# The channel table loaded in six pieces, and a new list of steps

## The chip, the cores and the metric

The kernel runs on one core of a Trainium2 chip. The metric is the device time of one execution in microseconds (us). Three executions of the kernel before took 529.64, 529.9 and 531.75 us; the median is 529.9 us.

## The reference

The reference is a gated linear attention (HGRN2) followed by a Fourier mixing block with a two-layer MLP. There are four batches, eight heads of 48 channels and 768 tokens; the eight heads make 384 channels.

```python
f = 1.0 / (1.0 + np.exp(-f_logit))
for t in range(S):
    state = f[:, :, t, :, None] * state + np.einsum('bhd,bhe->bhde', k[:, :, t], v[:, :, t])
    y[:, :, t] = np.einsum('bhd,bhde->bhe', q[:, :, t], state)
# heads side by side: x is (batch, 768, 384)
X = np.fft.fft(np.fft.fft(x, axis=1), axis=2)
u = x + np.real(X)
un = (u - mean(u)) / np.sqrt(var(u) + 1e-06)
out = u + np.maximum(un @ w_ch1, 0.0) @ w_ch2     # 384 -> 1536 -> 384
```

## The kernel before

**Work and stages.** Two heads make one unit, so there are 16 units, four to a batch. A unit runs through twelve or thirteen steps of the generator `attention`: the gate on ScalarE (L372, L373), a scan over the tokens on VectorE that gives the tile `W` (L379), exponentials on ScalarE (L383, L384, L387), two products on VectorE that turn q and k into scaled queries and keys (L391, L392), scores on TensorE (L400), a masked copy `at` on VectorE (L404), values and state sums `ds` on TensorE (L559, L599), a short scan `stt` over the chunk states on VectorE (L607), the state's part of the output (L616), a transpose back (L636), and `fold` on VectorE, which writes the even and odd parts `eo` (L663 to L669). The third and fourth unit of a batch also form the operands of the cosine transform there (`xs`, `xc`, `se`, `ce`, L678 to L687).

When the four units of a batch are folded, `fnet` does the Fourier transform with cosine and sine matrices: four products `z` with the sequence table `tab` (L725), then `mid` and `mix` with the channel table `cd` (L759, L744), and VectorE adds the result to x and takes the moments (L761 to L803). `turns` normalises a block of 128 tokens (`un`, L780) and transposes it (`pt`, L783; `unT`, L784), and `projected` does the MLP: for batch 0 with plain products `up` (L865) and `po` (L874), for the later batches with a fast matrix scheme (L836, L843), both followed by products `fx`, `fz` (L888). The tiles of `z`, `mid`, `mix`, `pt`, `up` and `po` share two PSUM buffers.

**Weights.** The MLP's weights arrive as 64-bit numbers in 24 blocks. `fetch` loads a block into one of three `raw` buffers (L310), and `weights` makes single precision of it with one instruction on ScalarE (L281), two on VectorE (L283, L284) and one on GpSimd (L285).

**What sets the order.** All steps stand in one list of words, `ORDER`, which a loop goes through (L951); each word issues its instructions to their engines' queues at once, and every queue then runs in that order. The scheduler adds only the waits. The words are: a bare number for the next step of that unit; `L` for loads of a unit (`L4qv`: q and v of unit 4); `K` for the turned keys of a unit; `r` for one fetch and `R` for three; `C` for one conversion of weights; `D` for eight filler matmuls on TensorE (L192); `T` for loading the tables and `S` for sorting them on GpSimd; `F`, `H` and `P` with a batch number for the next step of `fnet`, `turns` and `projected`; `B` and `W` for sums of weight blocks; `V` and `c` for a second look at the weights. `Z`, `I`, `i` and `M` set up and close.

**Loads.** All loads but the gather go through SyncE's queue. They take eight completion counters in turn, and a load whose counter is still in use waits, with all behind it, until the load eight before it has landed. A q, k or f load is 112 rows of 3 KB, issued as 96 and 16 rows; v is 360 KB and a weight block 384 KB. `tables` loads `tab` in four pieces (128, 15, 112 and 1 rows), has GpSimd gather its second half (L226, 395 KB), and loads the channel table into two tiles `wave` in three pieces. `sort_tables` then copies both into `cd` on GpSimd (L240 to L252).

```python
nc.sync.dma_start(out=wave[0][0:QD + 1], in_=dim_tab[0:QD + 1, 0])        # 97 rows, L232
nc.sync.dma_start(out=wave[1][0:63], in_=dim_tab[65:128, 1])              # 63 rows, L233
nc.sync.dma_start(out=wave[1][63:QD], in_=dim_tab[0:QD - 63, 2])          # 33 rows, L234
```

Of the kernel before, what the change touches and what calls it, by code (L numbers as in the profile page):

```python
# [12 lines left out]
C = 128  # L13
# [11 lines left out]


ORDER = (
    "Z I D L0f 0 i D L2f 2 D L1f D 1 L0q 0 L0k r D D D L1q 1 0 D D L0v L1k 0 L2q 2 C D 0 0 L2k 1 D D r 0 "
    "L3fk K0 D 1 1 K1 1 C 0 0 r 2 2 L1v D 3 D D r L3q 0 L2v L4fk 3 K2 C 1 0 C 1 1 3 2 1 D 2 3 3 4 2 0 L3v "
    "1 2 L5fk 5 D D 3 4 R 2 1 5 2 3 K3 C 4 3 L4qv 3 T D 2 L6fk 3 L5qv 5 C 4 D 2 4 4 3 3 4 S 2 3 C 5 K4 4 "  # L30
    "F0 F0 4 F0 F0 r C K5 5 6 r C 4 L6qv 5 F0 r r 4 5 L7fk H0 H0 r 5 H0 C 6 C 5 P0 7 P0 P0 r 6 C L7qv 6 "
    "P0 P0 5 C 6 K6 P0 r 6 7 C r P0 C P0 r r 7 C P0 F0 6 5 7 r r L9fk B C P0 P0 6 C 6 r r K7 C F0 P0 7 C "
    "7 C r 6 r H0 r C P0 P0 C 7 6 C P0 L8fk 7 H0 B L8qv 9 P0 P0 H0 B B 9 P0 8 7 P0 B 8 P0 9 B P0 P0 P0 8 "
    "P0 7 L9qv 4 9 9 K9 P0 B P0 5 8 P0 P0 7 H0 9 P0 7 9 8 B 9 H0 6 P0 P0 L11fk 9 11 W P0 6 P0 P0 9 K8 P0 "
    "P0 P0 B P0 P0 P0 P0 P0 8 7 P0 P0 P0 F1 P0 F1 L11qv P0 F1 F1 11 8 F1 P0 8 8 L10fk 10 P0 P0 P0 8 10 H1 "
    "P0 L10qv B P0 11 P0 P0 10 10 H1 B P0 P0 11 10 K10 P0 10 B 10 11 K11 11 L12fk B P0 H1 B B P1 P1 P1 P1 "
    "P1 B P1 P1 P1 P0 P1 P1 P1 P1 F1 P1 P1 F1 P1 P1 10 12 9 12 10 P1 P1 10 8 L12qv H1 9 P1 P1 12 12 10 P1 "
    "P1 H1 11 P1 12 11 H1 12 11 P1 P1 P1 H1 P1 P1 P1 P1 L13fk 13 P1 11 H1 P1 P1 P1 P1 P1 P1 P1 8 P1 P1 12 "
    "K12 L14fk 13 P1 14 P1 P1 12 L13qv 13 11 10 P1 13 12 10 P1 K13 11 P1 P1 P1 P1 P1 P1 14 P1 12 P1 11 P1 "
    "P1 P1 F2 F2 P1 14 P1 L14qv 14 F2 P1 P1 F2 P1 13 13 F2 13 K14 F2 F2 L15fk 13 13 P1 14 13 H2 P1 15 P1 "  # L40
    "15 P1 P1 L15qv 15 14 P1 14 P1 H2 14 15 H2 14 P1 P2 P2 P2 P2 H2 P2 P2 P2 P2 P2 P2 P2 P2 P2 P2 P2 13 "
    "14 15 H2 15 V 13 P2 K15 15 14 15 H2 V 14 15 P2 V P2 14 15 12 P2 P2 P2 15 12 c P2 H2 V P2 P2 P2 P2 P2 "
    "c 15 15 P2 P2 F3 F3 F3 P2 F3 P2 H2 P2 c P2 F3 P2 P2 F3 P2 c V F3 P2 P2 V P2 P2 P2 c c V V P2 P2 P2 "
    "H3 c P2 H3 P2 P2 P2 c P2 H3 P2 P2 P2 P2 P2 P2 P2 P2 V P2 P2 V P2 P2 P2 P2 V P2 P2 P2 c P2 c V c P2 V "
    "P3 c V P2 P3 P3 H3 V H3 P3 P3 P3 P3 P3 H3 P3 P3 P3 P3 P3 P3 P3 c V c c P3 c P3 V V P3 P3 P3 c P3 P3 "
    "P3 P3 P3 V P3 P3 H3 P3 P3 P3 P3 c c P3 V V V P3 P3 V P3 P3 P3 c c P3 P3 P3 P3 P3 P3 c V P3 P3 H3 c "
    "P3 c P3 P3 P3 M P3 P3 P3 P3 P3 P3 P3 P3 P3 P3 P3 P3 P3 P3 P3 P3 P3 P3 P3 P3"
)


# [33 lines left out]
def kernel(  # L84
# [13 lines left out]
    nc = tc.nc  # L98
    B, HP, _, D, _, S = qkf.shape
# [7 lines left out]
    QS, QD = S // 4, DM // 4  # L107
    R = 64 + D
# [106 lines left out]
    def tables():  # L215


        nc.sync.dma_start(out=tab[:, 0, 0], in_=seq_tab[:, 0, 0])
        nc.sync.dma_start(out=tab[1:16, 0, 1], in_=seq_tab[1:16, 0, 1])
        nc.sync.dma_start(out=tab[16:128, 0, 1], in_=seq_tab[16:128, 0, 1])  # L220
        nc.sync.dma_start(out=tab[0:1, 0, 1], in_=seq_tab[64:65, 1, 1])
        back = p1.tile([128, 1], U32, tag="most", name="back")
        nc.gpsimd.iota(back, pattern=[[0, 1]], base=1, channel_multiplier=3)
        nc.gpsimd.iota(back[64:128], pattern=[[0, 1]], base=3 * C + 1, channel_multiplier=-3)
        nc.gpsimd.iota(back[64:65], pattern=[[0, 1]], base=2, channel_multiplier=0)
        nc.gpsimd.indirect_dma_start(  # L226
            out=tab[:, 1].rearrange("p t m -> p (t m)"), out_offset=None,
            in_=seq_tab.rearrange("p j t m -> (p j) (t m)"),
            in_offset=bass.IndirectOffsetOnAxis(ap=back, axis=0))

        wave = [p2.tile([128, DM], F32, tag="un", name=f"wave{i}") for i in range(2)]
        nc.sync.dma_start(out=wave[0][0:QD + 1], in_=dim_tab[0:QD + 1, 0])  # L232
        nc.sync.dma_start(out=wave[1][0:63], in_=dim_tab[65:128, 1])  # L233
        nc.sync.dma_start(out=wave[1][63:QD], in_=dim_tab[0:QD - 63, 2])  # L234
        return wave

    def sort_tables(wave):
# [712 lines left out]
    with tc.manual_schedule():  # L950
        for word in ORDER.split():  # L951
            kind, n = word[0], int("0" + "".join(c for c in word if c.isdigit()))
# [14 lines left out]
            elif kind == "B":  # L967
                weight_sum()
            elif kind == "H":
                next(behind[n], None)  # L970
            elif kind == "r":
                fetch()
            elif kind == "V":
                reread()
            elif kind == "D":
                busy()
            elif kind == "C":
                weights()
            elif kind == "c":
                sizes()  # L980
            elif kind == "R":
                fetch(3)
            elif kind == "L":
                load(n, *word.strip("L0123456789"))
            elif kind == "I":
                start()
            elif kind == "i":
                nc.sync.dma_start(out=ident, in_=ident_in)
            elif kind == "T":
                wave = tables()  # L990
            elif kind == "S":
                sort_tables(wave)
            elif kind == "Z":
                zeros()
            elif kind == "M":
                flag = judge()
# [92 lines left out]
```

## Time and profile before

| What | Value |
|---|---|
| median of three executions | 529.9 us |
| the profiled execution's own time | 528.67 us |
| span of the profiled execution | 526.9 us |
| instructions | 13784 |
| TensorE (PE) busy | 497.4 us, 94% of the span |
| VectorE (DVE) busy | 379.6 us, 72% |
| ScalarE (ACT) busy | 224.8 us, 43% |
| GpSimd (POOL) busy | 58.0 us, 11% |
| moved by DMA | 48.15 MB, mean 91 GB/s |

The profiled execution is a fourth one; its span is 1.77 us shorter than its own time. Shares are means over a kernel with a loading stage, an attention stage and a long MLP stage, so they are read by stretches of time below, not as totals. In lines of a timeline the first number is the start, the second the duration (of a group: of the whole group), and the square brackets say how long the engine had stood idle before and what released it.

### The profile page before, as it was taken

What the parts mean: (1) busy time and instruction counts of PE and PEld (TensorE: products, weight loads), DVE (VectorE), ACT (ScalarE), POOL (GpSimd) and SP (SyncE); (2) the same over time, 40 slices, a digit from 0 to 9 for tenths busy, and PEclk for the clock granted to TensorE, in tenths of its full rate; (3) what the DMA queues carried; (4) which work ended last, traced back from release to release, by engine and by line L of the source; (5) the groups of instructions that cost most, each with busy time, mean ns of one, the idle gap of its engine ahead of it and who ended that gap; (6) DMA issues with size and microseconds to landing.
All of it is one profiled execution on the core that took longest, in us unless ns stands there. A gap on an engine that the chain in (4) does not pass through costs nothing.

```text
span 526.9 us, 13784 instructions
## 1 busy us (share of the span) xinstructions
PE 497.4 (94%) x5854; PEld 456.9 (87%) x5854; DVE 379.6 (72%) x746; ACT 224.8 (43%) x529; POOL 58.0 (11%) x85
## 2 busy tenths in 40 slices
PE   4867789999999999999999999999999999999995
PEld 4756668866899889999999889999899999999995
DVE  3777998998896258696598886686787566757561
ACT  6474667655530371444634534451441405132230
POOL 3110633351001000100001000000000000010000
PEclk9788899999999999999999999999999999999998
DMA  8998635674021121103031212110323112421101
GB/s 212 258 242 214 188 106 159 193 214 124 12 76 63 39 70 44 43 1 117 23 89 51 55 55 71 47 63 14 106 61 104 47 61 91 145 66 60 34 1 36
DMA packets 20462, 48.15 MB, mean 91 GB/s; under 512 B 3366, under 2 KB 5991, under 8 KB 20391
## 3 DMA queue, kind: packets, MB, share of 16 engines
q1 hardware_dynamic: 19142, 43.43, 29.5%
q0 software_dynamic: 1104, 3.54, 1.8%
q8 instruction: 48, 0.79, 0.6%
q14 instruction: 24, 0.19, 0.1%
q10 hardware_dynamic: 144, 0.20, 0.1%
HBM read 42.44 MB, written 4.72 MB: 89 GB/s over the span
## 4 chain that ended last, share of the span: by engine, by line
PE 81%; DVE 9%; issue 1%; ACT 1%; DVEq 0%
PE ub L836 24%; PE fx L888 16%; PE fz L888 12%; PE up L865 7%; PE z L725 3%; PE po L874 3%; PE y L559 3%; PE mix L744 2%; PE pt L783 2%; PE ds L599 2%; DVE w L284 2%; PE y L616 2%; PE yt L636 1%; PE sc L400 1%; PE st L538 1%
## 5 line engine op out<-in xcount | busy, mean ns | idle before, releaser
L843 DVE TENSOR_TENSOR h<-h,ub 128x512 f32<-128x512 f32 x81 | 55.1, 686 | 40.4 <-PE ub L836 40.3
L692 POOL DMA_INDIRECT out_dram<-x,place x16 | 17.8, 1112 | 383.5 <-DVE x L918 261.6
L841 ACT ACTIVATE h<-ub 128x512 f32<-128x512 f32 x54 | 32.2, 597 | 58.6 <-PE ub L836 58.1
L865 PE MATMUL up<-unT,w 128*128 128x256 f32 x216 | 49.3, 381 | 0.6 <-ACT unT L784 0.6
L845 ACT ACTIVATE h<-h 128x512 f32<-128x512 f32 x54 | 33.9, 631 | 33.3 <-DVE h L843 33.3
L888 PE MATMUL fx<-block,h 128*128 128x192 f32 x264 | 46.6, 327 | 0.0
L836 PE MATMUL ub<-unT,w 128*128 128x128 f32 x360 | 46.6, 280 | 0.0
L865 PEld LDWEIGHTS up<-unT,w 128*128 128x128 f32 x216 | 40.2, 190 | 6.3 <-ACT unT L784 0.8
L888 PE MATMUL fx<-w,h 128*128 128x192 f32 x264 | 45.4, 327 | 0.0
L836 PEld LDWEIGHTS ub<-unT,w 128*128 128x128 f32 x360 | 43.2, 191 | 0.7
L888 PEld LDWEIGHTS fx<-block,h 128*128 128x128 f32 x264 | 43.3, 190 | 0.1
L888 PEld LDWEIGHTS fx<-w,h 128*128 128x128 f32 x264 | 42.7, 190 | 0.3 <-ACT unT L784 0.2
L836 PE MATMUL ub<-wide 128*128 128x128 f32 x288 | 39.0, 281 | 0.0
L836 PE MATMUL ub<-wide,w 128*128 128x128 f32 x288 | 38.2, 280 | 0.0
L285 POOL TENSOR_TENSOR w<-w,raw 128x384 uint32<-128x384 uint32 x24 | 27.2, 1132 | 75.9 <-DVE w L284 39.1
L836 PEld LDWEIGHTS ub<-wide 128*128 128x128 f32 x288 | 34.6, 191 | 1.0 <-issue 0.4
L836 PEld LDWEIGHTS ub<-wide,w 128*128 128x128 f32 x288 | 34.3, 191 | 1.1 <-DVE h L843 0.3
L379 DVE TENSOR_TENSOR_SCAN W<-g,bound 112x768 f32<-112x768 f32 x12 | 21.0, 1750 | 9.2 <-ACT g L373 9.2
L784 ACT COPY unT<-pt 128x384 f32<-128x384 f32 x24 | 11.6, 487 | 35.8 <-PE pt L783 35.8
L867 ACT ACTIVATE h<-up 128x256 f32<-128x256 f32 x36 | 13.5, 380 | 30.3 <-PE up L865 30.3
L559 PE MATMUL y<-at,v 64*48 64x64 f32 (+1 forms) x768 | 19.3, 229 | 6.6 <-DVE at L404 2.9
L559 PEld LDWEIGHTS y<-at,v 64*64 64x64 f32 (+1 forms) x768 | 15.6, 135 | 10.3 <-issue 4.1
(188 smaller groups left out, 1003.0 us busy)
## 6 DMA issues: line engine op xcount, KB each, us to landing
raw<-in_w_ch_dram SPq DMA_DIRECT2D x24, 384.0 KB, 6.1
v<-in_v_dram SPq DMA_DIRECT2D x16, 288.0 KB, 4.5
k<-in_w_ch_dram SPq DMA_DIRECT2D x12, 384.0 KB, 3.7
g<-in_w_ch_dram SPq DMA_DIRECT2D x12, 384.0 KB, 3.4
k<-in_qkf_dram SPq DMA_DIRECT2D x14, 288.0 KB, 4.0
g<-in_qkf_dram SPq DMA_DIRECT2D x12, 288.0 KB, 6.4
q<-in_qkf_dram SPq DMA_DIRECT2D x12, 288.0 KB
wide<-in_qkf_dram SPq DMA_DIRECT2D x10, 288.0 KB, 5.4
```

The source lines that it names most:

```text
L285: nc.gpsimd.tensor_tensor(bits, bits, lo, ALU.add)
L379: nc.vector.tensor_tensor_scan(W, g, bound[:R], 0.0, ALU.add, ALU.min)
L559: nc.tensor.matmul(y[FILL[g], c // 3, c % 3 * C + t.start:c % 3 * C + t.stop], lhsT=vals[rows, o:o + (64 if g == 0 else D)], rhs=weights, ...
L692: nc.gpsimd.indirect_dma_start(out=out.rearrange("b s d -> (b s) d"), out_offset=bass.IndirectOffsetOnAxis(ap=place[:, b, i:i + 1], axis=0 ...
L725: nc.tensor.matmul(z[:, cols], lhsT=src[:, j, lo:hi], rhs=tab[:, t, T % 2, cols], start=(i == 0), stop=(i == len(parts) - 1), skip_group_c ...
L836: nc.tensor.matmul(banks[bank][:, m * 128:(m + 1) * 128], lhsT=block(w)[:, m * 128:(m + 1) * 128], rhs=tokens(a), start=(new and m == 0), ...
L841: nc.scalar.activation(out, got, AF.Copy, scale=1.0 if how == "=+" else -1.0)
L843: nc.vector.tensor_tensor(out, out, got, ALU.add if how == "+" else ALU.subtract)
L845: nc.scalar.activation(out, out, AF.Relu)
L865: nc.tensor.matmul(pp[:, :256], lhsT=w1[:, kt, m * 128:(m + 1) * 128], rhs=unT[:, kt], start=(kt == 0), stop=(kt == 2))
L874: nc.tensor.matmul(po[:, :DM], lhsT=h[:, m, t], rhs=w2[:, m], start=(m == 0), stop=(m == NF - 1))
L888: nc.tensor.matmul(out, lhsT=h[:, m], rhs=blocks[i][:, m], start=(start and m == 0), stop=(m == H - 1), skip_group_check=True)
```

## The change

The change does two things. The channel table is loaded in six pieces in place of three: 96 and 1 rows, then 48 and 15, then 32 and 1. The rows land in the same places. And `ORDER` is another list: it holds the same 720 words, each as often as before, in another sequence. Of the list, the part up to the first words of the MLP is shown. All six pieces carry line number 234 in the new kernel.

```diff
 ORDER = (
-    "Z I D L0f 0 i D L2f 2 D L1f D 1 L0q 0 L0k r D D D L1q 1 0 D D L0v L1k 0 L2q 2 C D 0 0 L2k 1 D D r 0 "
-    "L3fk K0 D 1 1 K1 1 C 0 0 r 2 2 L1v D 3 D D r L3q 0 L2v L4fk 3 K2 C 1 0 C 1 1 3 2 1 D 2 3 3 4 2 0 L3v "
-    "1 2 L5fk 5 D D 3 4 R 2 1 5 2 3 K3 C 4 3 L4qv 3 T D 2 L6fk 3 L5qv 5 C 4 D 2 4 4 3 3 4 S 2 3 C 5 K4 4 "
-    "F0 F0 4 F0 F0 r C K5 5 6 r C 4 L6qv 5 F0 r r 4 5 L7fk H0 H0 r 5 H0 C 6 C 5 P0 7 P0 P0 r 6 C L7qv 6 "
-    "P0 P0 5 C 6 K6 P0 r 6 7 C r P0 C P0 r r 7 C P0 F0 6 5 7 r r L9fk B C P0 P0 6 C 6 r r K7 C F0 P0 7 C "
+    "L0f Z L2f L0k 0 2 I r 0 i 0 L0q D r D D D C 0 L0v D D L1f D C 0 1 0 D L2q D 1 0 L1q L1v K0 0 D 2 L1k "
+    "D D r r D 1 1 C D L2k T 0 D 2 1 L3q L3fk D 1 0 C K1 L4fk L2v 0 2 1 2 1 3 L5fk S 0 2 R 4 1 K2 3 4 "
+    "L3v 1 3 3 2 C 5 D 2 2 5 L4qv C 1 4 3 D D 3 2 K3 3 4 1 r 2 L5qv 3 3 D 5 2 3 L6fk 3 5 4 D 4 K5 "
+    "K4 3 2 4 3 C 5 C 4 r F0 4 C r F0 L7fk 6 F0 5 F0 C 4 r F0 4 5 H0 H0 5 C H0 P0 r 6 r L6qv C 5 L7qv P0 "
+    "6 P0 r C r 6 P0 C 5 r C 6 P0 r 7 6 F0 P0 7 6 C K6 P0 r B C C r P0 P0 7 r F0 6 P0 7 P0 6 C L8fk "
...
@@ tables
-        nc.sync.dma_start(out=wave[0][0:QD + 1], in_=dim_tab[0:QD + 1, 0])
-        nc.sync.dma_start(out=wave[1][0:63], in_=dim_tab[65:128, 1])
-        nc.sync.dma_start(out=wave[1][63:QD], in_=dim_tab[0:QD - 63, 2])
+        for w, o, n, rows in ((0, 0, QD, dim_tab[:, 0]), (0, QD, 1, dim_tab[QD:, 0]), (1, 0, 48, dim_tab[65:, 1]),
+                              (1, 48, 15, dim_tab[113:, 1]), (1, 63, 32, dim_tab[:, 2]), (1, 95, 1, dim_tab[32:, 2])):
+            nc.sync.dma_start(out=wave[w][o:o + n], in_=rows[:n])
```

In the queues this means: the tables' loads (`T`) come right after the k load of unit 2 and ahead of q, f and k of unit 3, where they came after v of unit 4; the gather on GpSimd follows the third conversion of weights instead of the fifth; the keys of unit 0 and two weight blocks are loaded before the f of unit 1; and from the first `F0` on the two lists differ by shifts of a few words. The sum of the second weight blocks (`W`) comes after 238 words in place of 276.

## The prediction

> **What bounds the kernel now.** I read the busy table by stretches first, with borders where its character changes (columns: span of the stretch, then PE, PE weight loads, DVE, ACT and POOL busy, clock, DMA share, GB/s).
>
> ```profile
> 0.00:36.00 36.00, 23.66 (x541) 21.23 (x545) 20.82 (x26) 22.37 (x40) 8.87 (x33) 0.90 0.97 234
> 36.00:82.00 46.00, 36.05 (x829) 29.50 (x821) 40.01 (x79) 26.40 (x76) 13.82 (x21) 0.89 0.64 177
> 82.00:109.00 27.00, 26.18 (x356) 22.50 (x356) 26.20 (x39) 18.81 (x45) 12.29 (x10) 1.00 0.61 179
> 109.00:521.00 412.00, 411.51 (x4140) 383.67 (x4140) 292.24 (x606) 157.18 (x370) 22.97 (x21) 1.00 0.21 64
> ```
>
> To 36 us the DMA engines are full (0.97) and VectorE is busy 20.82 of 36; to 82 us VectorE is the fullest engine (40.01 of 46, 87%); from 82 us TensorE is full and VectorE nearly so; from 109 to 521 us TensorE misses 0.5 us. TensorE's work after 82 us is fixed, so the end moves with the start of the first `up` at 82.16, and with what TensorE loses later. The waits of VectorE up to 82 us name what it lacked:
>
> ```profile
> DVE W L379 <- ACT g L373: 8.9, 2, 6.2
> DVE stt L607 <- PE ds L599: 5.9, 4, 2.9
> DVE at L404 <- PE sc L400: 2.6, 2, 2.3
> DVE un L780 <- ACT rstd L771: 1.0, 1, 1.0
> DVE W L379 <- DMA wide<-in_qkf_dram: 0.6, 1, 0.6
> ```
>
> That is 19.0 us, of which 6.23 is the wait for the first f. The chain of waits from 53 to 109 us is mostly VectorE's lines, so its queue sets the first `up`. Third, SyncE's queue around the channel table:
>
> ```profile
> 45.04 0.23 SPq L232 DMA_DIRECT2D wave<-in_dim_tab_dram  x1
> ...
> 48.50 0.42 SPq L212 DMA_DIRECT2D q<-in_qkf_dram  x1
> 54.52 0.31 SPq L213 DMA_DIRECT2D q<-in_qkf_dram  x1
> ```
>
> The 16-row piece of q for unit 5 waits 5.6 us for the 97-row load eight places ahead, which lands 9.25 us after its issue end (54.52 less 45.27). Nothing pays: unit 5 uses q at 69.15 without a wait, and no engine waits for a weight block until 105 us (0.36).
>
> [...] 145.5 KB in 9.25 us is 16 KB/us, where all engines move about 241. [...] L284 takes 0.56 us alone and 1.26 beside L285. [...]
>
> **The change, part by part.** *The split.* Three loads become six: three more issues of some 0.42 us, 1.3 us of SyncE's queue. It removes a 5.6 us stall that is hidden now. In the new place, at about 27 us, that stall would not be hidden, so the split pays for the move.
>
> *Work up to the first `up`.* Both lists hold the same words before the first `P0` but for three: the new one leaves one fetch, `stt` of unit 5 (0.75) and the scan of unit 6 (1.75 and 0.80) for later. TensorE's work ahead is equal, fillers too.
>
> *When data land.* A load that waits for its counter dates the landing eight places ahead: f of unit 2 (688 KB in all) by 6.97 us, q of unit 2 (3448 KB) by 18.41. So 241 KB/us: landing = 4.1 us + KB/241. The tables agree (10.65 MB, 48.3 us by rule; landed about 46 to 49). On the new list: first weight block 9.9, q0 11.5, second block 13.1, f1 16.0, k1 21.7, k2 26.3, tables and channel table 29.1, with the gather (1.6) q3 32.1, f3 33.5, f4 36.3, f5 40.5, then two weight blocks 43.6 and 45.2, q4 49.6. The tables (386, 290 and 395 KB, 4.4 us of DMA) now stand ahead of f3.
>
> *VectorE's queue, walked with those landings and the durations of before* (scan and L380 1.95, product 1.0, `at` 1.0, `stt` 0.75, conversion 0.9, `eo` 2.4). First scan 6.23 as before, to 8.2; conversion waits for its block, 9.9 to 10.8; q0 at 11.5, k product to 13.5; conversion 14.4; `at` 15.5. Scan of unit 1 waits for f1 and two ACT passes of 0.85: 17.7. Two scans 21.5, products 23.5, conversion, `stt`, `at`, conversion, products of unit 2: 29.1. `eo` of unit 0 31.9, `at` 32.9, `stt` 33.7. The scan of unit 3 waits for f3 (33.5 and 1.7): 35.2 to 37.1. Scan of unit 4 (f4 and 1.7) 38.0 to 40.1; products of unit 3 40.5 to 42.5. Conversion waits for its block: 43.6 to 44.5; `stt`, scan of unit 5 (ACT, 45.9), conversion, `at`, products of unit 4 51.9; `eo`, `stt`, `eo`, products of unit 5, `at`, `eo` 63.0; transform operands (4.0) 67.0. Before, they ended at 68.3 with unit 5's products (2.6) still to do. The waits sum to 15.5 us against 18.0 at the same point: **2.5 us less**, mainly because a conversion, an `eo` and a scan fill what were holes.
>
> Then four conversions (0.9, and three beside GpSimd at 1.26), `stt` and `at`: 6.4 us, so 73.4 for the row addition L761, which stood at 75.72. TensorE is ready sooner: `se` at 64.8, four `z` of 1.45, a `y` of 0.87, `mid` 0.5, copies between: 72. From L761 to the first `up` 6.44 us as before; one more conversion sits in the 1.02 us wait for `rstd`. First `up` at 79.85: **2.3 us earlier**.
>
> *After it.* TensorE lost 0.83 us at 109 us, where `po` waited for L803 of the third `mix`, for its PSUM buffer. From L761 to that L803 VectorE now has three products' and additions' steps of `mix` and `un` (7.9 us, `rstd`'s wait in it), two scans (4.6), eight conversions (nine less the one ahead, 8.7), `stt`, two products, `at` and a weight sum (4.4), 25.6 in all: 99.0, and with the 0.8 us of gaps that 82 to 109 us shows now, 99.8. TensorE has from the first `up` nine `up` of 1.31, two `mix` of 1.49, two `y`, an `sc` and turned keys (3.1), so the third `mix` ends at 97.7, and after a `y` with `ds` (1.7) and one more `up` it asks for that buffer at 100.7. The wait goes: **0.8 us**. `W` moved up by 38 words puts 5.4 us (four of 1.36) earlier on VectorE; it is hidden as long as TensorE holds as much independent work, and `po` and three `up` behind it (2.0 and 1.3 each), a `y` and an `sc` (0.87 each) are 7.6 us. If that cover is gone it costs up to 5.4.
>
> Sum: -2.3 - 0.8 = -3.1. On the profile's own time 528.67 gives 525.6; the median stands 1.2 above that run, so 529.9 gives **526.8 us**. About 0.5% (2.65 us) is what a measurement of this kernel can tell from no change.
>
> **Costs that the trace does not show.** The six pieces' landings in their new place: from no cost (the rule holds) to 2.2 us if ten table loads of 0.5 us each hold the counters while they carry 676 KB (5.0 us against 2.8). I take none and keep 2.2 for the range. [...]
>
> **The rivals.** *Landings run late: slower.* From the scan of unit 3 on, five waits of my walk (1.5, 0.9, 0.4, 1.1, 0.6) end on landings; each us by which f3, f4 and the two weight blocks are late goes to the first `up` in full. For it: ten narrow loads stand directly ahead, with the DMA share at 1.0. Against it: before, the same ten took 40.17 to 46.55. At 3.1 us beyond the rule nothing is left; at 5.8 the kernel is slower by 0.5%. With 6.5 us late: 533.3. *Nothing that can be measured.* The stall was hidden, [...]: 528.8. *A larger gain.* Between 10 and 30 us the DMA engines now move 254 KB/us; if landings run ahead of my rule and those five waits go, VectorE's queue is 4.5 us earlier still, at L761 and at L803 alike: 522.3. That the split itself does nothing is the second case: it alone, at the old place, would give 529.9.
>
> **How the numbers follow.** The forecast is a gain of 1.5 to 4.7 us, 525.2 to 528.4 as its own range, chance 0.48; the bound of 2.65 cuts it at a third (0.32 faster, 0.16 same). The larger gain has 0.20, since my walk gave every landing its full delay; nothing measurable 0.12; late landings 0.20. So faster 0.52, same 0.28, slower 0.20. For 8 in 10 I reach from somewhat below the larger gain's value, 521.5, to the late landings, 533.5.
>
> **What would show it.** Right: no wait of SyncE's queue on `wave`; the first `up` near 80 us; `un` near 76; no wait of `po` on L803; TensorE at 99% from there. Wrong: scans of units 3 and 4 after 37 and 40 us, by DMA; holes in TensorE of over 1 us after 100 us (on `at`, or on VectorE's additions around `W`); or the first `up` early and the end unmoved.

## Result and the profile after

The change made no difference that the measurement can tell. Twelve executions of the changed kernel have a median of 529.62 us, twelve of the kernel before in the same rounds 529.77 us; the ratio is 0.9994, with a 95% interval of 0.997 to 1.0019. Two later sets gave 1.0059 (1.0036 to 1.0081) and 0.9997 (0.9977 to 1.0017), so taken together it is no gain, and perhaps 0.2% slower. The forecast was 526.8 us, with "faster" as the likeliest class: no gain of that kind is there.

The profiled execution of the changed kernel took 530.86 us (span 529.1), 1.2 us above its median; that of the kernel before took 528.67 us. The busy table of the changed kernel, with the same borders as in the prediction (span of the stretch, then PE, PE weight loads, DVE, ACT and POOL busy, clock, DMA share, GB/s):

```profile
0.00:36.00 36.00, 24.31 (x565) 21.49 (x565) 24.07 (x33) 20.33 (x38) 15.10 (x49) 0.90 0.89 239
36.00:82.00 46.00, 36.96 (x807) 30.51 (x808) 40.70 (x79) 31.01 (x84) 9.64 (x8) 0.90 0.71 197
82.00:109.00 27.00, 26.89 (x354) 21.53 (x352) 26.01 (x42) 19.10 (x48) 10.43 (x10) 1.00 0.63 185
109.00:521.00 412.00, 409.25 (x4128) 381.52 (x4128) 286.83 (x594) 154.23 (x361) 20.35 (x18) 1.00 0.20 61
```

VectorE does 3.3 us more of its work before 36 us (24.07 against 20.82), and from 82 to 109 us TensorE is busy for 26.89 us in place of 26.18: the wait of `po` on L803 is gone. But from 109 to 521 us, where TensorE missed 0.5 us, it now misses 2.75 us. The waits of VectorE up to 82 us (us in total, times, longest) fell from 19.0 to about 14.7 us; the largest:

```profile
DVE W L379 <- ACT g L373: 8.8, 3, 6.6
DVE stt L607 <- PE ds L599: 1.8, 1, 1.8
DVE eo L663 <- ACT x L641: 1.4, 1, 1.4
DVE W L379 <- ACT wide L373: 1.1, 1, 1.1
```

SyncE's queue has no wait on `wave` any more. The timeline of the changed kernel's TensorE then shows the gain, and where it went:

```profile
78.94 5.45 PE L865 MATMUL up<-unT,w 128*128 128x256 f32 x24 [0.57 <-ACT unT L784]
...
113.42 0.85 PE L599 MATMUL ds<-v,kT 128*64 128x48 f32 x20
116.14 0.52 PE L783 MATMUL pt<-ident,un 128*128 128x128 f32 x3 [1.87 <-DVE un L780]
```

The first `up` starts 3.2 us earlier than the 82.16 of before. At 114.3 us TensorE has done all that stands ahead of the turn of chunk 1 (a chunk is a block of 128 tokens; its `un` on VectorE, then its `pt`, L783) and waits 1.87 us for VectorE's `un`. VectorE's timeline just ahead of it:

```profile
109.10 0.86 DVE L780 TENSOR_SCALAR un<-x,mv,rstd 128x384 f32<-128x384 f32 x2
111.08 0.36 DVE L283 TENSOR_SCALAR w<-raw 128x384 uint32<-128x384 uint32 x1 [1.12 <-DMA raw<-in_w_ch_dram]
111.47 1.26 DVE L284 SCALAR_TENSOR_TENSOR w<-raw,w 128x384 uint32<-128x384 uint32 x1
113.86 1.15 DVE L283 TENSOR_SCALAR w<-raw 128x384 uint32<-128x384 uint32 x1 [1.14 <-DMA raw<-in_w_ch_dram]
115.04 0.56 DVE L284 SCALAR_TENSOR_TENSOR w<-raw,w 128x384 uint32<-128x384 uint32 x1
115.52 0.47 DVE L780 TENSOR_SCALAR un<-x,mv,rstd 128x384 f32<-128x384 f32 x1
```

The last two conversions of weights stand ahead of that `un`, and each waits 1.1 us for its block. The chain of waits names what they wait for; its columns are start, duration and piece:

```profile
106.77 1.02 POOL w L285
107.79 0.02 issue
107.81 6.04 DMA raw<-in_w_ch_dram
113.84 0.02 issue
113.86 1.16 DVE w L283
```

The last block's fetch had to wait until GpSimd's addition freed one of the three `raw` buffers, and then took 6.04 us. The kernel before has its last conversions at much the same time, but TensorE still had `po` to do there. Its lines (the first is the wait on L803 that the prediction wanted to remove):

```profile
109.17 4.11 PE L874 MATMUL po<-w,h 128*128 128x384 f32 x12 [0.83 <-DVE x L803]
...
114.69 2.11 PE L874 MATMUL po<-w,h 128*128 128x384 f32 x6
118.36 0.55 PE L783 MATMUL pt<-ident,un 128*128 128x128 f32 x3
```

```profile
116.25 0.99 DVE L283 TENSOR_SCALAR w<-raw 128x384 uint32<-128x384 uint32 x1 [0.38 <-DMA raw<-in_w_ch_dram]
```

It missed nothing at this `pt`; in four later profiles with the old order of the rest it waits 0.4 to 0.6 us there.

A second loss follows in this execution. The clock in stretches of 2 us after the hole:

```profile
114.00:116.00 2.00, 0.27 (x6) 0.08 (x2) 1.97 (x4) 0.57 (x1) 1.06 (x2) 1.00 0.12 35
116.00:118.00 2.00, 1.86 (x11) 1.51 (x12) 0.66 (x1) 1.30 (x3) 0.87 (x1) 0.83 0.03 8
118.00:120.00 2.00, 2.00 (x4) 1.01 (x3) 1.08 (x1) 1.44 (x4) 0.00 (x0) 0.50 0.00 0
120.00:122.00 2.00, 2.00 (x6) 1.14 (x5) 1.92 (x5) 1.00 (x2) 0.00 (x0) 0.81 0.00 0
```

The `po` products, which cover this time, are 17.7 us busy in place of 16.2, so 1.5 us went to the clock. How long a hole was does not tell whether a low clock followed it: the one of 1.87 us stood ahead of the 0.50 here, and after those of 1.23 (`after_again`), 1.49 (`list_alone`), 1.50 (`third_fourth_unread`), 1.88 (`table_later`) and 2.09 us (`third_sum_first`) in five other runs below the clock was 1.00.

### The profile page after: what moved, and what is told of

Same layout as the page of the kernel before. It is cut to its first block, busy times and chain, and to the rows that moved or that the text cites. A ratio compares the mean times of both kernels' runs of the same rounds, so it can differ in the third digit from the quotient of the medians.

```text
span 529.1 us, 13793 instructions
## 1 busy us (share of the span) xinstructions
PE 498.8 (94%) x5854; PEld 456.2 (86%) x5854; DVE 378.2 (71%) x746; ACT 224.7 (42%) x529; POOL 56.5 (11%) x85
## 4 chain that ended last, share of the span: by engine, by line
PE 80%; DVE 4%; DMA 2%; issue 1%; ACT 1%; POOL 0%; DVEq 0%
PE ub L836 24%; PE fx L888 16%; PE fz L888 12%; PE up L865 8%; PE z L725 3%; PE mix L744 3%; PE y L559 2%; PE po L874 2%; DMA raw<-in_w_ch_dram 2%; PE sc L400 2%; PE pt L783 2%; PE y L616 1%; PE ds L599 1%; PE yt L636 1%; PE st L538 1%
## 5 line engine op out<-in xcount | busy, mean ns | idle before, releaser
L836 PE MATMUL ub<-wide 128*128 128x128 f32 x288 | 38.3, 280 | 0.1
L285 POOL TENSOR_TENSOR w<-w,raw 128x384 uint32<-128x384 uint32 x24 | 28.5, 1189 | 74.9 <-DVE w L284 38.1
L888 PE MATMUL fz<-w,h 128*128 128x192 f32 x132 | 23.6, 328 | 0.0
```

The source lines that it names most:

```text
L285: nc.gpsimd.tensor_tensor(bits, bits, lo, ALU.add)
L836: nc.tensor.matmul(banks[bank][:, m * 128:(m + 1) * 128], lhsT=block(w)[:, m * 128:(m + 1) * 128], rhs=tokens(a), start=(new and m == 0), ...
L888: nc.tensor.matmul(out, lhsT=h[:, m], rhs=blocks[i][:, m], start=(start and m == 0), stop=(m == H - 1), skip_group_check=True)
```

## The experiments

My theory after this comparison, "given back": the front gains, and TensorE loses it again at the turn of chunk 1, because the last weight blocks are late. Rivals: the hole costs nothing on the whole; the combination `W` costs; the profiled front was luck; the split itself matters. Ratios are to the kernel before in the same set of runs, with the 95% interval.

**Part by part.** `split_alone` is the old list with the six pieces, `list_alone` the new list with the three old ones.

> The old list with the six pieces of the wave. Theory 'given back': the 5.6 us wait of the queue behind the 97-row piece goes, but it was hidden there, so the time is that of the kernel before within 0.7 us (529.1 to 530.5). Rival 'the split pays by itself': the first up product comes 2 to 3 us earlier than 82.2 us and the time falls to about 527. Rival 'three more issues cost': the queue's later loads come 2 us later, and the time rises to about 531.5.

> The new list with the three old pieces. Theory 'given back': the 97-row piece needs about 9 us where the list now puts it at 22 us, the queue stands behind it for 3 to 6 us, and the loads of units 3 and 4 come that much later: first up at 81 to 84 us, the time 531 to 534 us. Rival 'the split is idle': loads have that much slack, first up at 79 us and the time that of the changed kernel within 0.7 us.

`split_alone`: 1.0009 (0.9989 to 1.003), first `up` at 81.2 us. At the old place the split changes nothing that these runs can tell, as the hidden stall said. `list_alone`: 1.0036 (1.0021 to 1.0051), first `up` at 82.86 us; the waits of SyncE's queue to 82 us show the stall at the new place:

```profile
SPq L213 <- DMA wave<-in_dim_tab_dram: 5.8, 1, 5.8
```

It holds the second piece of unit 3's k load until 33.4 us, and unit 4's loads behind it. The stall is real there; what the six pieces bring over it is not told from the scatter of the changed kernel's three sets (0.9994 to 1.0059).

**The list in two halves.** `new_front_old_rest` takes the new list's first 151 words, to the first `P0`, and the remaining words in their old order; `old_front_new_rest` the reverse, with the old pieces.

> The changed kernel's list up to its first word of the up products (151 words), and from there the words that are left in the order of the kernel before, with the six pieces. Theory 'given back': first up at about 79 us, no hole of TensorE over 1 us between 82 and 130 us, and 526.6 us (529.8 less 3.2). Rival 'the front's gain is never worth its 3 us later, whatever the rest is': 529 to 530 us, with other waits of TensorE that add up to 3 us after 82 us.

> The kernel new_front_old_rest once more, on the chip and beside the runs of these others. If its 0.22% is real: 0.997 to 0.999 of the kernel before; if the chip or the session made it, 1.000 to 1.003 like third_sum_first, which differs from it in one word. First up anywhere from 79 to 83.5 us.

> The list of the kernel before up to its first word of the up products, and from there the words that are left in the new order, with the three old pieces. Theory 'the front is worth 1.2 us and the new rest costs as much': first up at 81 to 83 us, a hole of TensorE before pt on L783 at 115 to 121 us, and a time 0.7 to 2.5 us above the kernel before (529.7 to 531.5). Rival 'the new rest costs nothing': the time of the kernel before within 0.5 us.

`new_front_old_rest` gave 0.9978 (0.9959 to 0.9996) and, in another set, 0.9988 (0.9967 to 1.001): 0.6 to 1.2 us gained, with no hole over 0.85 us after 82 us. Its first `up` came at 83.35 and 81.7 us, not at 79. So a gain of the front is likely, but it is about 1 us and not 3, and only the first of the two intervals lies below 1. `old_front_new_rest` took 1.0154 (1.0124 to 1.0183), far off what either theory expected: TensorE waits 3.3 us at 92 us for an `sc` that a weight block releases, with the clock at 0.50 from 94 to 96 us, and 1.0 us for `un` at 123.7. The two halves depend on each other; what the new rest costs by itself is not to be had from it.

**The turn ahead of the late conversions.**

```diff
-... C H0 P0 H0 C 7 L9qv C H0 9 ...
+... C H0 P0 H0 H0 C 7 L9qv C 9 ...
```

> The turn of chunk 1 (un on L780, pt on L783) stands ahead of the last two conversions of weights in place of behind them; nothing else differs from the changed kernel. Theory 'given back': TensorE's hole of 1.87 us before pt at 116 us goes, and with it the low clock (0.83, 0.50, 0.81) of the 6 us after it, some 1.6 us; together 3.4 us, so about 526.2 us, with a granted clock of 1.00 from 112 to 122 us. Rival 'hole is harmless': the hole moves to the next product that needs a late block, and the time stays at 529 to 530 us. Rival 'W': the cost lies with the combination W on VectorE at 124 to 129 us, and this kernel stays within 0.5 us of the changed one.

> The kernel with the turn of chunk 1 ahead of the last two conversions once more, now timed beside the changed kernel on the same chip. Theory 'given back': 1.5 to 3 us below the changed kernel in the same rounds, hole at most 0.6 us, clock 1.00 from 110 to 124 us. Rival 'the hole costs nothing on the whole': within 0.7 us of the changed kernel.

> The changed kernel itself, a second execution under the profiler and more timed ones. Theory 'given back': the hole of TensorE before pt on L783 at 114 to 120 us is there again (1 to 2.5 us, with or without the low clock after it), while the first up product may come anywhere from 79 to 83 us, since three executions with the same first 151 words had it at 78.9, 80.3 and 83.3; the median stays within 1 us of the kernel before. Rival 'the profiled execution was an oddity': no hole over 0.6 us, and the median 1.5 us or more below the kernel before.

`turn_first` gave 1.0014 (0.9991 to 1.0037). In a later set, beside the changed kernel at 1.0059, it gave 1.0035 (1.0004 to 1.0066), 1.2 us less by the medians, with intervals that overlap. In both profiles the hole shrinks to 0.57 us and the clock stays at 1.00, as expected; the time does not fall by the 3.4 us that the recorded profile had promised. `after_again`, the changed kernel itself, explains part of it: its hole is 1.23 us, with no low clock after it, so there was less to win.

**One wait more of the old rest.** In `new_front_old_rest` the third sum (`F0`) is put ahead of a conversion.

```diff
-... K7 C F0 P0 7 C ...
+... K7 F0 C P0 7 C ...
```

> As new_front_old_rest, and in it the front's third sum (the word F0 of L800 and L803) stands ahead of one conversion of weights in place of behind it, so that x on L803 is ready about 1.6 us earlier. Theory: the wait of 0.8 us of po on L803 goes, and the time falls by that below new_front_old_rest, to about 526.7 us, clear of the kernel before by 0.4%. Rival 'the weight stream sets the pace': po starts earlier but TensorE waits as much later, for the last block of w or for un, and the time is that of new_front_old_rest (527.5).

1.0023 (0.9998 to 1.0048), from the set in which every kernel with the new front came out high. The wait of `po` on L803 went, and a wait of 2.09 us before `pt` came in its place at 119 us, as the rival said: TensorE is earlier, the last block is not.

**The front: whose landing?** Unit 3's loads stand behind the ten table pieces. Two runs with the same first 151 words, the changed kernel and then `turn_first_2`, in SyncE's timeline:

```profile
21.90 3.83 SPq L234 DMA_DIRECT2D wave<-in_dim_tab_dram  x6
25.78 0.31 SPq L212 DMA_DIRECT2D wide<-in_qkf_dram  x1
```

```profile
24.41 4.78 SPq L234 DMA_DIRECT2D wave<-in_dim_tab_dram  x6
29.24 0.31 SPq L212 DMA_DIRECT2D wide<-in_qkf_dram  x1
```

The queue is 2.5 us behind at `wave` and 3.5 us at unit 3's loads, by many small waits for loads eight places ahead (in the first of the two, up to 82 us, none is over 1.2 us); the first `up` comes at 78.94 and 83.15 us. `table_later` moves the word `T` behind `L3q L3fk`; two others join that with `turn_first` and with the old rest.

> The changed kernel with the word T (the four table pieces and the six wave pieces) behind the loads of unit 3's q, f and k in place of ahead of them, nothing else. Theory 'unit 3's landing sets the front': the loads of unit 3 are issued at about 18 us in place of 26 to 29, the scan of its wide on L379 starts at about 31 us in place of 34.4 to 38.3, the wait of W on ACT's wide (1.1 to 3.8 us) goes, and the first up product comes 1.5 to 3 us earlier than the 81.1 us that is the mean of six executions, at 78 to 79.5 us, with little scatter. The hole before pt on L783 stays, so the time falls by 1 to 2.5 us below the changed kernel. Rival 'the front is set elsewhere': first up at 80 to 83 us, the time as the changed kernel. Rival 'the weight stream sets the pace': first up earlier, but the hole before L783 grows by as much, the time as the changed kernel.

> The edit of table_later and that of turn_first together. If both places count, as 'given back' has it: first up at 78 to 79.5 us, hole before L783 at most 0.6 us, and 1.5 us below the kernel before, about 527.5 us or less. Rival 'the weight stream': the hole comes back at the turn or at the last products of po, 529 us or more.

> The edit of table_later in new_front_old_rest. 'Given back': first up at 78 to 79.5 us, the wait of po on L803 of 0.8 us stays, and the time is 1.5 to 3 us below the kernel before, 526 to 527.5 us. Rival 'the weight stream': the last conversions come no earlier than 117 us, TensorE waits 2 us or more ahead of L783 or L874 there, and the time is within 1 us of the kernel before.

The loads went out at 18 us as meant, and nothing came of it: first `up` at 81.2, 82.4 and 80.1 us. The wait moved on to the next operand in ScalarE's timeline of `table_later`:

```profile
32.17 0.85 ACT L372 ACTIVATE wide<-wide 112x768 f32<-112x768 f32 x1
36.42 0.84 ACT L372 ACTIVATE g<-g 112x768 f32<-112x768 f32 x1 [2.43 <-DMA g<-in_qkf_dram]
```

Unit 3's f is there without a wait; unit 4's reaches ScalarE at 36.4 us (36.8 and 33.7 in the other two), where nine executions with the changed front as it was have 36.0 to 39.1. The ratios are 1.0028 (1.0007 to 1.0049), 1.0001 (0.9981 to 1.0021) and 0.9982 (0.9963 to 1.0). My expectation of the front was a miss. The set shows something else: with the same front, new rest and old rest differ by 2.2 us (530.60 and 528.39, intervals apart), and `turn_first`'s edit takes some 1.75 us of that back (528.85, intervals that overlap).

**Taking landings away.** A fetch is left out and its conversion reads the block before.

```diff
-raws.append(words(len(raws)))
+raws.append(raws[-1] if len(raws) in (2, 3) else words(len(raws)))    # or (22, 23), or all four
```

> The changed kernel without the fetches of the third and fourth weight blocks (L310; two transfers of 393 KB that are issued at 15 to 17 us, just ahead of unit 3's loads); the conversions stay and read the second block's data, so these two blocks of w hold wrong values. Theory 'the front is bound by what the transfers carry': 0.79 MB less is 3.3 us at 241 KB per us, unit 3's wide reaches ACT's L372 at 29 to 32 us in place of 32.5 to 36.5, the first up product comes at 77.5 to 79.5 us against a mean of 81.1, and the time falls by 1.5 to 3 us below the changed kernel of the same call. Rival 'the front is bound by VectorE and TensorE': first up at 80 to 82.5 us, the time within 0.7 us of the changed kernel.

> The changed kernel without the fetches of the last two weight blocks; their conversions stay where they are, ahead of un on L780, and read the data of the block before, so these two blocks of w hold wrong values. Theory 'given back to late blocks': VectorE's two waits of 1.1 us on raw go, un of chunk 1 comes 2 to 4 us earlier, TensorE's hole before pt on L783 is at most 0.3 us, and the time falls by 1.2 to 2.5 us below the changed kernel of the same call. Rival 'order and not landing': VectorE is too full there in any case, the hole stays over 1 us, and the time within 0.7 us of the changed kernel.

> The third, the fourth and the last two fetches left out together, conversions kept; four blocks of w hold wrong values. If front and hole are two separate losses, their gains add: first up at 77.5 to 79.5 us, no hole over 0.3 us, and 3 to 5 us below the changed kernel of the same call. If the gain of the front is eaten by what follows whatever the last blocks do, the time is that of last_two_unread within 0.7 us.

> The changed kernel once more, beside these three. Theory: first up anywhere from 79 to 83.5 us, a hole of 1 to 2.2 us before pt on L783, and a median 0 to 2.5 us above the kernel before, as in its two sets so far (0.15 us below it, and 2.7 us above).

In one set: the changed kernel 0.9997 (0.9977 to 1.0017), 529.34 us; without the third and fourth fetch 0.995 (0.9931 to 0.997), 527.39 us; without the last two 0.998 (0.9958 to 1.0003), 528.85 us; without all four 0.993 (0.9909 to 0.9951), 526.55 us. So 768 KB less in the first 17 us are worth 2.0 us (intervals apart): these two transfers do hold up the front. Whether by their bytes or by their places in SyncE's queue is not told apart, since both go with the fetch; that moving loads within the same stretch did nothing speaks for the bytes. The last two are worth 0.5 us, which is not resolved by itself; all four together bring 2.8, so nothing speaks against the two losses being separate. In `four_unread` the first `up` is the earliest of all:

```profile
76.83 5.45 PE L865 MATMUL up<-unT,w 128*128 128x256 f32 x24 [0.57 <-ACT unT L784]
```

And although TensorE is that early, it has no hole before L783: VectorE, in the same order, reaches `un` at 110.60 us, since no conversion waits. So it is the landing that makes the hole, not the order alone. `last_two_unread` has none either, with a first `up` at 82.60 us.

`after_third`, the changed kernel once more, has no hole with a first `up` at 80.70 us; the conversion of its last block waits for nothing:

```profile
115.17 0.85 PE L599 MATMUL ds<-v,kT 128*64 128x48 f32 x20
115.96 0.53 PE L783 MATMUL pt<-ident,un 128*128 128x128 f32 x3
```

```profile
114.47 0.36 DVE L283 TENSOR_SCALAR w<-raw 128x384 uint32<-128x384 uint32 x1
```

Three executions of the changed kernel had their first `up` at 78.94, 79.30 and 80.70 us, and the turn of chunk 1 at 116.14, 116.18 and 115.96 us. By these alone the turn has a date of its own, which eats what the front gains. Two other kernels with the new rest and all their blocks contradict that: they are late in front and have the hole all the same. `table_later` and then `list_alone`:

```profile
81.21 5.45 PE L865 MATMUL up<-unT,w 128*128 128x256 f32 x24 [0.57 <-ACT unT L784]
...
118.45 0.52 PE L783 MATMUL pt<-ident,un 128*128 128x128 f32 x3 [1.88 <-DVE un L780]
```

```profile
82.86 5.45 PE L865 MATMUL up<-unT,w 128*128 128x256 f32 x24 [0.57 <-ACT unT L784]
...
119.38 0.52 PE L783 MATMUL pt<-ident,un 128*128 128x128 f32 x3 [1.49 <-DVE un L780]
```

This is the key to the case. In all five the fetch of the last block is issued 28.6 to 28.9 us after the first `up`: it moves with the front. It then takes 5.6 to 6.1 us to land in the four with a hole, and at most 4.9 us in `after_third`. So the hole takes the new rest and a slow last block, and not an early front: it came in four of these five executions, with the first `up` at 78.94 us as at 82.86. "Given back" has the place and the block right, and the reason wrong.

Against the old rest, the whole loss is some 1.5 to 2 us. From the first `up` to the start of the last group of products, four executions with the new rest and an undisturbed clock there take 437.7 to 439.4 us (mean 438.7), three with the old rest and every block 436.4 to 437.4 (mean 436.9), and the two controls below, with blocks left out, 437.2 and 438.0. The 2.2 us between `table_later` and `table_later_old_rest` are the same loss in timed runs. Removing the hole, by the order or by leaving out the last blocks, gave 0.5, 0.8, 1.2 and 1.75 us by the medians, no one of them resolved by itself.

**Controls in the kernel before**, with the same fetches left out of its own list.

> Control in the kernel before (old list, three old pieces): the fetches of its third and fourth weight blocks left out, conversions kept, two blocks of w wrong. In the changed kernel the same cut brought 2.0 us. Theory 'both fronts are bound by what the transfers carry in the first 40 us': first up at 78 to 80.5 us in place of 81.2 to 82.5, and 1 to 3 us below the kernel before. Rival 'the old front waits for TensorE, not for transfers': first up at 81 to 82.5 us, the time within 0.7 us of the kernel before.

> Control in the kernel before: the fetches of its last two weight blocks left out, conversions kept, two blocks of w wrong. In the old order TensorE has six products of po as cover there, so the theory 'only the new order lays the late blocks open' has no hole to close: 0 to 0.7 us below the kernel before. Rival 'late blocks cost the old order as much': 1 us or more below it.

`old_third_fourth_unread`: 0.9985 (0.9962 to 1.0008), first `up` at 79.4 us in its profile; a gain is likely and not proved. `old_last_two_unread`: 1.0012 (0.9994 to 1.003): late last blocks cost the old order nothing that these runs can tell, where `po` covers them.

No version clearly beat both kernels: the best that fetch every block, `table_later_old_rest` and `new_front_old_rest`, stand at 0.998 to 0.999.

## Why the prediction was wrong

*The split: right.* The stall was hidden at the old place (`split_alone`), and 5.8 us long and open at the new one (`list_alone`). The profile before shows only that the 97 rows (145.5 KB) took 9.25 us; that 96, 48 and 32 rows would land sooner was not shown there. In the profile after no load waits for a piece of `wave`, and the one piece whose landing is timed, the 32 rows (48 KB), took 3.5 us.

*First `up` 2.3 us earlier: right direction, mis-sized.* The recorded profile flattered it (78.94 for the 79.85 forecast). Nine executions with the changed front and its transfers whole had it at 78.9, 79.3, 80.3, 80.7, 81.4, 81.7, 82.6, 83.15 and 83.35 us, mean 81.3; four with the old front at 81.2, 81.7, 82.2 and 82.5, mean 81.9. The gain is 0.6 us by these, which their scatter does not resolve, and 0.6 to 1.2 by the times of `new_front_old_rest`. One term that failed is the landing rule: 4.1 us + KB/241, read off one execution, was taken as a date for each load. In the nine runs the scan of unit 3 started between 34.4 and 38.3 us (forecast 35.2). "Landings run late" was a rival with 0.20; it was part of the ordinary case. A second term stands nowhere in the prediction: the clock. The four earliest of the nine (mean 79.8, the forecast) have no low clock between 50 us and the first `up`, and need 44.0 to 44.6 us from the scan of unit 3 to that product; the five others have a stretch at 0.50 there, and need 44.8 to 46.0. All four with the old front have such a stretch between 56 and 68 us, and so has the profile that the forecast was built on:

```profile
64.00:66.00 2.00, 1.93 (x43) 1.52 (x35) 1.97 (x5) 0.03 (x1) 1.91 (x2) 0.50 0.61 183
```

No run sets late landings and low clock apart. So how much of the front's missing 1 to 2 us is due to which stays open.

*The wait of `po` on L803: right.* The 0.8 us are in none of the profiles with the whole new list.

*`W` is covered: right.* TensorE's only wait of over 0.5 us after 82 us is the one on `un`.

*"TensorE at 99% from there": wrong, and it decided.* The step "After it" followed L803 and `W`, and stopped there. The weight blocks were walked no further than the first `up`; that no engine waited for one until 105 us was taken as slack for the rest. In the new order the last two conversions are in front of a turn for which TensorE has no other work, and it waits 1.2 to 1.9 us there in four executions of five. The prediction named the sign (holes over 1 us after 100 us) but not the cause, and gave "the first `up` early and the end unmoved" no mechanism of its own; it had 0.12 with two other reasons.

*"TensorE's work after 82 us is fixed": wrong by about 1.3 us.* The products from the first `up` to the last group are the same ones. With waits of over 0.15 us taken off, they need 435.5 to 436.3 us in six profiles with the old rest and 436.7 to 437.4 in eight with the new one, all at an undisturbed clock. It is the order and not scatter: by the start times of the groups, `fx` and `fz` together take 150.7 us in all twelve profiles with the new rest and 149.6 in all eight with the old one, and the `sc` of L576 takes some 0.4 more. Which neighbours make them dearer was not tried.

*Smaller terms.* The prediction counts three words that the new list leaves for after the first `P0`; there are four, the loads of q and v of unit 6 being the other. In the profile before TensorE waits twice for nothing that the profile shows ("issue"), 1.96 us (ends 34.25) and 1.97 us (ends 46.75); the longest such wait up to 82 us in the profile after is 0.41 us (ends 24.95), and in `after_third`, the same kernel, one of 2.38 us ends at 27.99. The cause is not shown.

The sum by what the runs showed: about 0.6 to 1.2 us gained in front; in the rest 1.3 lost on TensorE's own products, 0 to 1.9 lost in the hole, 0.8 gained on L803, and once 1.5 lost to the clock. That is nothing, or slightly slower.

## What to carry to other kernels

Here, with the DMA engines' share at 0.97 (before) and 0.89 (after) in the first 36 us, moving loads within that stretch only shifted the wait to the next operand (2.43 us for unit 4's f in `table_later`); taking 768 KB out of it brought 2.0 us (`third_fourth_unread`). Before an early gain is booked, walk every stream (here the weight blocks with their three buffers) to the point where its consumers meet it: that nothing waits for a stream in one order does not mean that it has slack in another, because the work that covers it may have been moved. Compare a suspected loss across executions with early and late starts before calling it the price of the early start. And read landings, and the clock, off several executions; one profile can be the lucky one.

## What was unexpected in the hardware

The same instructions landed their data up to 4 us apart by 36 us into the kernel (unit 3's f reached ScalarE at 32.5 to 36.5 us in nine executions, on several chips; three of them on one chip had 33.3, 33.6 and 36.5), and single executions of one kernel differ by over 7 us (527.03 to 534.44 among the twelve of the changed kernel). A low clock came at quite different places. Every one of the twenty profiles has at least two stretches at about half clock (0.50) before 50 us, and fifteen have another between 50 and 86 us. From 86 to 516 us only two have one, each right after a wait of TensorE: the recorded one at 116 to 122 us, after 1.87 us, and `old_front_new_rest` at 92 to 98 us, after 3.27 us. In `third_fourth_unread`, whose own time was 530.75 us against a median of 527.39, the clock is at 0.50 from 74 to 84 us, and fell some 2 us after a wait of 1.30 us:

```profile
76.00:80.00 4.00, 3.43 (x52) 2.67 (x45) 3.65 (x5) 1.19 (x3) 2.43 (x1) 0.50 0.93 275
80.00:84.00 4.00, 4.00 (x11) 3.08 (x10) 1.59 (x4) 0.91 (x2) 0.57 (x1) 0.50 0.44 127
```
